# An mLSTM cell in front of a mixture layer: attention in halves of 64 tokens, in 64x64 quadrants of TensorE, with a state between the halves

## The chip, the cores and the metric

The kernel runs on one core of one Trainium2 chip. The metric is the device time in microseconds (us) of one execution; less is better. All times below come from one profiled execution of the kernel before, unless they are called a median.

## The reference

Two layers, one behind the other. The first is an mLSTM cell over 768 tokens, for 4 batches of 8 heads (32 pairs of batch and head) with head size 40:

```python
for t in range(S):
    m_new = np.maximum(f_gate[:, :, t] + m, i_gate[:, :, t])
    f_stab = np.exp(f_gate[:, :, t] + m - m_new)
    i_stab = np.exp(i_gate[:, :, t] - m_new)
    m = m_new
    C = f_stab[:, :, None, None] * C + i_stab[:, :, None, None] * np.einsum('bhd,bhe->bhde', vt, kt)
    n = f_stab[:, :, None] * n + i_stab[:, :, None] * kt
    h_tilde = np.einsum('bhde,bhe->bhd', C, qt)
    nq = np.einsum('bhd,bhd->bh', n, qt)[:, :, None]
    y[:, :, t] = o * h_tilde / np.maximum(np.abs(nq), 1.0)   # o = sigmoid(o_gate)
```

The second layer takes the 3072 tokens of 320 features (8 heads of 40):

```python
h = x @ w_in                                  # 320 -> 2048
out = (h * (1 / (1 + np.exp(-1.702 * h)))) @ w_out   # 2048 -> 320
```

The recurrence over tokens can be cut into windows. Within a window it is an attention with a causal mask and weights exp(...) from the gates; what came before the window enters through a state C (with n as a 41st column), which is brought forward once a window.

## The kernel before

**Windows.** There are 6 windows `w` of 128 tokens. A window has two stages. The *up* stage computes w_in times the tokens of all four batches (512 columns) for 16 blocks of 128 hidden features (`p_h`, L390 and L396) and applies the GELU on ScalarE (L401). The *down* stage multiplies by w_out: in window 0 straight, in 16 blocks (`p_out`, L417); from window 1 on as 14 products of a Strassen-like scheme (`down_fast`, L471), each 8 matmuls of 128x160, which needs sums of hidden blocks (`hidden_sums`, L452 to L456) and additions of the products into `o_sb` (L474, L476), all on VectorE.

**Attention.** The attention of window w+1 is spread over the down stage of window w, by `attention()`, one list of steps, and `stops`, the blocks behind which a step is issued. Each step serves one batch b (8 heads, as 4 pairs `p` of heads; head i of a pair lies in rows i*64 to i*64+39 of the transposed keys and queries):

- `columns`: the gate rows (`st`, from `gates`) are transposed by TensorE into columns `p_cols`, copied (L266) and put through exp (L267, L269); then the output gate's tanh (L271).
- `weights`: 8 exps on ScalarE (L305) over a tile `wt` into which `spread` has loaded the gate row from memory, one for each head; then the causal mask on POOL (L307, an affine select of 128x1024).
- `scores`: 8 matmuls K^T Q of 40 rows, two heads in the two row tiles of the array (`p_s`, L315), multiplied into `wt` by VectorE (L317).
- `values`: `p_o` = wt times V, 8 matmuls of 128x41 (L325), and `p_i` = Q times the state, 4 matmuls for pairs of heads (L330); VectorE scales and adds (L334, L335), divides and applies the gate (L338 to L344).
- `seam`: three transposes of the result (`p_x`, L353), copied by ScalarE into `xT` (L354), which the next up stage reads.

`carry` brings the state forward: POOL multiplies V by gate columns (`vw`, L360), TensorE multiplies by the keys (`p_c`, L364), POOL decays the old state (L371), VectorE adds (L375). It stands in the up stage of its own window, one batch behind each of the first four `j`. `transposes` of window w+1 stand behind the last four `j`: 8 TensorE transposes a batch (`p_t`, L279), keys copied by ScalarE and queries by VectorE (L281).

**Order.** Every engine runs its instructions in the order in which the program issues them (the schedule is written by hand), and waits in that order. So what stands behind a waiting instruction on an engine waits with it. All loads and stores go through SyncE's queue: `load` (L97), `load_gates` (L89), `fetch` (L137), `spread` (L287), stores (L422, L480). Products in float32 leave two records for each matmul in the profile, transposes one.

**Accumulators.** `ps_a` has four buffers of one bank, for all of attention; `ps_m` has four, for the mixture layer.

Of the kernel before, what the change touches and what calls it, by code (L numbers as in the profile page):

```python
# [17 lines left out]

L = 128
NEG = -1.0e30


# [7 lines left out]
def kernel(  # L34
# [24 lines left out]
    DH = DM // 2  # L59
    assert BH == 32 and D <= DP and DM == 320 and W == 512 and B == 4 and S % L == 0 and NF == 16  # L60
# [9 lines left out]
    ps_a = ctx.enter_context(tc.tile_pool(name="ps_a", bufs=4, space=PSUM))  # L70
# [7 lines left out]
    q_st = const.tile([L, BH, DP], FP, name="q_st")  # L78
    k_st = [const.tile([L, BH, DP], FP, name=f"k_st{i}") for i in range(2)]
# [6 lines left out]
    def load_gates(w):  # L86
        for dst, src in ((f_sb, f_gate), (i_sb, i_gate)):
            dst[w] = ld.tile([BH, L], FP, tag="fi", bufs=4, name="fi")
            nc.sync.dma_start(out=dst[w], in_=src[:, :, w * L:(w + 1) * L].rearrange("b h s -> (b h) s"))  # L89

    def load(w, what, bs=slice(0, B)):
        hs = slice(bs.start * H, bs.stop * H)
        for c in what:
            if c == "o" and w not in eo:
                eo[w] = ld.tile([L, BH, D], FP, tag="eo", bufs=1, name="eo")
            dst, src = {"k": (k_st[w % 2], k), "q": (q_st, q), "v": (v_st, v), "o": (eo.get(w), o_gate)}[c]
            nc.sync.dma_start(out=dst[:, hs, 0:D],  # L97
                              in_=src[bs, :, w * L:(w + 1) * L, :].rearrange("b h s d -> s (b h) d"))
# [39 lines left out]

    load_gates(0)
# [8 lines left out]

# [37 lines left out]
    for t in (k_st[0], q_st):  # L186
        G.memset(t[:, :, D:DP], 0.0)
# [3 lines left out]
    state = const.tile([128, BH // 2, 2, D1], FP, name="state")  # L191
# [5 lines left out]
    kT, qT, wt, ys, xT, gs, o_ps, sums = {}, {}, {}, {}, {}, {}, {}, {}  # L197
# [16 lines left out]
    def gates(w):  # L214
# [35 lines left out]
        V.tensor_scalar(out=st[BH:2 * BH, :], in0=m_run, scalar1=m, scalar2=None, op0=OP.subtract)  # L250
        V.tensor_scalar(out=st[2 * BH:3 * BH, :], in0=a, scalar1=end, scalar2=-1.0, op0=OP.subtract, op1=OP.mult)
        if 0 < w < NW - 1:
            dec[w] = gate.tile([BH, BH // 2], FP, name="dec")
            both = gate.tile([BH, 1], FP, name="both")
            V.tensor_tensor(out=both, in0=m, in1=end, op=OP.subtract)
            V.tensor_scalar(out=dec[w], in0=pair, scalar1=both, scalar2=None, op0=OP.mult)

    def columns(w):
        pt = ps_a.tile([L, 3 * BH + BH // 2], FP, tag="a", name="p_cols")
        T.transpose(pt[:, 0:3 * BH], stacked[w], ident[0:3 * BH, 0:3 * BH])  # L260
        n = 3 * BH
        if w in dec:
            n += BH // 2
            T.matmul(pt[:, 3 * BH:n], half.rearrange("p a b -> p (a b)"), dec[w], start=True, stop=True)
        c = cols[w] = gate.tile([L, 3 * BH + BH // 2], FP, name="cols")
# [8 lines left out]
    def transposes(w, b):  # L274
        for src, dst, name, copy in ((k_st[w % 2], kT, "kT", A.copy), (q_st, qT, "qT", V.tensor_copy if w else A.copy)):
            pt = ps_a.tile([128, NP, L], FP, tag="a", name="p_t")
            for p in range(NP):
                h = b * H + 2 * p
                T.transpose(pt[:, p, :], src[:, h:h + 2, :].rearrange("p a b -> p (a b)"), ident)  # L279
            dst[w, b] = work.tile([128, NP, L], FP, tag=name, bufs=4, name=name)  # L280
            copy(out=dst[w, b], in_=pt)  # L281

    def spread(w):

        for b in range(B):
            x = wt[w, b] = work.tile([L, NP, 2, L], FP, tag="wt", bufs=4, name="wt")
            nc.sync.dma_start(out=x.rearrange("s p i t -> s (p i) t"),  # L287
                              in_=m_row[w][b * H:(b + 1) * H, :].unsqueeze(0).to_broadcast([L, H, L]))

    def weights(w, b):  # L290
        if w == 0:
            x = wt[w, b] = work.tile([L, NP, 2, L], FP, tag="wt", bufs=4, name="wt")
            for i in range(2):
                pw = ps_a.tile([L, NP, L], FP, tag="a", name="p_w")
                T.matmul(pw, ident_b, neg_mask.unsqueeze(1).to_broadcast([L, NP, L]), start=True, stop=False)
                for p in range(NP):
                    h = b * H + 2 * p + i
                    one = pick[:, h:h + 1].to_broadcast([3 * BH, L])
                    T.matmul(pw[:, p, :], one, m3, start=False, stop=False)
                    T.matmul(pw[:, p, :], a3, one, start=False, stop=(p == NP - 1))  # L300
                A.activation(out=x[:, :, i, :], in_=pw, func=AF.Exp)
            return
        x = wt[w, b].rearrange("s p i t -> s (p i) t")
        for h in range(H):
            A.activation(out=x[:, h, :], in_=x[:, h, :], func=AF.Exp, scale=-1.0,  # L305
                         bias=cols[w][:, b * H + h:b * H + h + 1])
        G.affine_select(out=x, in_=x, compare_op=OP.is_ge, fill=0.0, base=0, pattern=[[0, H], [1, L]],  # L307
                        channel_multiplier=-1)

    def scores(w, b):  # L310
        pw = [ps_a.tile([L, NP, L], FP, tag="a", name="p_s") for _ in range(2)]
        for p in range(NP):
            for i in range(2):
                r = slice(i * 64, i * 64 + D)
                T.matmul(pw[i][:, p, :], kT[w, b][r, p, :], qT[w, b][r, p, :], start=True, stop=True)  # L315
        for i in range(2):
            V.tensor_tensor(out=wt[w, b][:, :, i, :], in0=pw[i], in1=wt[w, b][:, :, i, :], op=OP.mult)  # L317

    def values(w, b):
        hs = slice(b * H, (b + 1) * H)  # L320
        po = ps_a.tile([L, H, D1], FP, tag="a", name="p_o")
        for p in range(NP):
            for i in range(2):
                h = 2 * p + i
                T.matmul(po[:, h, :], wt[w, b][:, p, i, :], v_st[:, b * H + h, :], start=True, stop=True)  # L325
        u = po
        if w:
            pi = ps_a.tile([L, H, D1], FP, tag="a", name="p_i")
            for p in range(NP):
                T.matmul(pi[:, 2 * p:2 * p + 2, :].rearrange("p a b -> p (a b)"), qT[w, b][:, p, :],  # L330
                         state[:, b * NP + p].rearrange("p a b -> p (a b)"), start=True, stop=True)
            u = work.tile([L, H, D1], FP, tag="u", name="u")
            g = cols[w][:, BH + b * H:BH + (b + 1) * H].unsqueeze(2).to_broadcast([L, H, D1])
            V.tensor_tensor(out=u, in0=pi, in1=g, op=OP.mult)  # L334
            V.tensor_tensor(out=u, in0=po, in1=u, op=OP.add)  # L335

        den = work.tile([L, H, 1], FP, tag="den", name="den")
# [5 lines left out]
        y = ys[w, b] = work.tile([L, DM + 64], FP, tag="y", name="y")  # L343
        V.scalar_tensor_tensor(out=y[:, 0:DM].rearrange("p (h d) -> p h d", d=D), in0=z, scalar=0.5,  # L344
                               in1=den.to_broadcast([L, H, D]), op0=OP.mult, op1=OP.mult)
        G.tensor_copy(out=y[:, DM:DM + 64], in_=y[:, DM - 64:DM])

    def seam(w, b):
        if b == 0:
            xT[w] = work.tile([128, 3, B, L], FP, tag="xT", bufs=1, name="xT")  # L350
        px = ps_a.tile([128, 3, L], FP, tag="a", name="p_x")
        for c in range(3):
            T.transpose(px[:, c, :], ys[w, b][:, c * 128:(c + 1) * 128], ident)  # L353
        A.copy(out=xT[w][:, :, b, :], in_=px)  # L354

    def carry(w, b):
        hs = slice(b * H, (b + 1) * H)
        vw = work.tile([L, H, D1], FP, tag="vw", name="vw")
        e = cols[w][:, 2 * BH + b * H:2 * BH + (b + 1) * H].unsqueeze(2).to_broadcast([L, H, D1])
        G.tensor_tensor(out=vw, in0=v_st[:, hs, :], in1=e, op=OP.mult)  # L360
        pc = ps_a.tile([128, NP, 2, D1], FP, tag="a", name="p_c")
        for p in range(NP):
            h = b * H + 2 * p
            T.matmul(pc[0:64 + D, p].rearrange("p a b -> p (a b)"),  # L364
                     k_st[w % 2][:, h:h + 2, :].rearrange("p a b -> p (a b)")[:, 0:64 + D],
                     vw[:, 2 * p:2 * p + 2, :].rearrange("p a b -> p (a b)"), start=True, stop=True)
        ps = slice(b * NP, (b + 1) * NP)
        if w:
            d = cols[w][:, 3 * BH + b * NP:3 * BH + (b + 1) * NP].unsqueeze(2).to_broadcast([128, NP, 2 * D1])
            old = state[:, ps].rearrange("p j a b -> p j (a b)")  # L370
            G.tensor_tensor(out=old, in0=old, in1=d, op=OP.mult)  # L371
        for i in range(2):
            r = slice(i * 64, i * 64 + D)
            if w:
                V.tensor_tensor(out=state[r, ps, i, :], in0=pc[r, :, i, :], in1=state[r, ps, i, :], op=OP.add)  # L375
            else:
                V.tensor_copy(out=state[r, ps, i, :], in_=pc[r, :, i, :])
# [45 lines left out]

# [62 lines left out]


    def attention(w):
# [124 lines left out]
```

## Time and profile before

| | |
|---|---|
| median of 3 runs | 569.14 us (568.95 to 569.47) |
| span of the profiled execution | 567.2 us |
| median less that span | 2.0 us |
| TensorE busy | 557.2 us (98%) |
| VectorE, ScalarE, POOL busy | 254.8, 179.5, 64.4 us |
| up stage of window 1 (132.88 to 175.27) | 42.4 us |
| down stage of window 1 (175.27 to 223.9) | 48.6 us |

The span is the time from the first to the last instruction in the trace; 2.0 us of the measured time lie around it. The profile's parts that matter are the busy shares of the engines; the chain of work that ended last, which is followed back from the last instruction and is also given piece by piece in order of time; the timeline, which lists groups of instructions with their start, length and what ended the idle time before them; and the waits, which say in total which engine waited in front of which line, and for whom. PE is TensorE's matmul side, PEld its weight loads, DVE VectorE, ACT ScalarE, SP SyncE.

### The profile page before, as it was taken

The numbers are of one execution on the slowest core, as the hardware profiler recorded it, in microseconds if no ns is written. First come the engines' busy times: TensorE is split into PE (matmuls) and PEld (weight loads), VectorE is DVE, ScalarE is ACT, GpSimd is POOL, SyncE is SP. The second block draws the span as 40 slices with busy tenths as digits, with TensorE's granted clock in tenths as the row PEclk, the third lists the DMA queues.
The fourth block names the chain that finished last, engine by engine and source line by source line (L and its number), as shares of the span: only waits on it lengthen the run. The fifth ranks groups of instructions, "written<-read, shape, count | busy, mean of one in ns | idle before, by whom it ended". The sixth has DMA issues, their size and how long they took to land.

```text
span 567.2 us, 8277 instructions
## 1 busy us (share of the span) xinstructions
PE 557.2 (98%) x3282; PEld 401.7 (71%) x3282; DVE 254.8 (45%) x583; ACT 179.5 (32%) x387; POOL 64.4 (11%) x103
## 2 busy tenths in 40 slices
PE   8989999999999999999999999999999999999997
PEld 5844556885548998456999544899745699944697
DVE  6755869532645445016454314545302644400611
ACT  5544668102233420322610213441033262022200
POOL 5011001102400202100110210021210011000000
PEclk9979999999999999999999999999999999999999
DMA  9789699003654002581300392400342000000000
GB/s 167 148 263 206 167 304 110 1 23 72 150 92 50 24 1 51 73 189 22 39 13 1 72 219 23 49 24 2 71 94 102 0 13 13 12 14 0 0 24 24
DMA packets 111959, 41.45 MB, mean 73 GB/s; under 512 B 100624, under 2 KB 106800, under 8 KB 111920
## 3 DMA queue, kind: packets, MB, share of 16 engines
q1 hardware_dynamic: 111920, 40.92, 35.8%
q8 instruction: 26, 0.43, 0.3%
q14 instruction: 13, 0.11, 0.1%
HBM read 36.90 MB, written 4.01 MB: 72 GB/s over the span
## 4 chain that ended last, share of the span: by engine, by line
PE 88%; SPq 4%; DVE 3%; DMA 2%; ACT 1%; issue 1%; DVEq 0%; ACTq 0%
PE p_h L390 29%; PE p_out L471 28%; PE p_h L396 8%; PE p_o L325 6%; PE p_s L315 4%; PE p_out L417 4%; PE p_i L330 3%; PE p_t L279 3%; PE p_c L364 3%; SPq L137 2%; SPq L97 2%; PE p_x L353 1%; DMA bits<-in_moe_w_out_dram 1%; DVE w_out_sb L211 1%; DVE w_out_sb L209 1%
## 5 line engine op out<-in xcount | busy, mean ns | idle before, releaser
L390 PE MATMUL p_h<-xT,w_in_sb 128*128 128x512 f32 x384 | 178.2, 609 | 2.8 <-ACT xT L354 2.8
L390 PEld LDWEIGHTS p_h<-xT,w_in_sb 128*128 128x128 f32 x384 | 70.4, 192 | 94.5 <-issue 88.0
L401 ACT ACTIVATE g<-p_h 128x512 f32<-128x512 f32 x96 | 54.8, 596 | 147.7 <-PE p_h L396 86.3
L471 PE MATMUL p_out<-w_out_sb,g 128*128 128x160 f32 x480 | 70.5, 300 | 0.0
L471 PEld LDWEIGHTS p_out<-w_out_sb,g 128*128 128x128 f32 x480 | 66.7, 190 | 1.0 <-issue 0.5
L354 ACT COPY xT<-p_x 128x384 f32<-128x384 f32 x24 | 11.5, 478 | 148.8 <-PE p_x L353 148.8
L305 ACT ACTIVATE wt<-wt,cols 128x128 f32<-128x128 f32 x160 | 48.0, 392 | 0.0
L471 PE MATMUL p_out<-t,s 128*128 128x160 f32 x320 | 47.9, 303 | 0.0
L396 PE MATMUL p_h<-xT,w_in_x 64*128 64x512 f32 x192 | 47.7, 615 | 0.0
L325 PEld LDWEIGHTS p_o<-v_st,wt 128*128 128x128 f32 x384 | 45.0, 192 | 1.6 <-DVE wt L317 0.8
L325 PE MATMUL p_o<-v_st,wt 128*128 128x41 f32 x384 | 45.4, 278 | 0.6 <-DVE wt L317 0.6
L307 POOL TENSOR_SCALAR_AFFINE_SELECT wt<-wt 128x1024 f32<-128x1024 f32 x20 | 21.9, 1096 | 208.4 <-ACT wt L305 208.4
L476 DVE TENSOR_TENSOR o_sb<-o_sb,p_out 128x160 f32<-128x160 f32 x70 | 21.4, 317 | 53.8 <-PE p_out L471 53.6
L471 PEld LDWEIGHTS p_out<-t,s 128*128 128x128 f32 x320 | 44.2, 190 | 1.1
L281 DVE COPY qT<-p_t 128x512 f32<-128x512 f32 x20 | 13.7, 687 | 55.8 <-PE p_t L279 55.8
L375 DVE TENSOR_TENSOR state<-p_c,state 40x164 f32<-40x164 f32 x32 | 10.4, 326 | 60.2 <-PE p_c L364 59.5
L396 PEld LDWEIGHTS p_h<-xT,w_in_x 64*128 64x128 f32 x192 | 16.5, 186 | 29.5 <-issue 28.5
L317 DVE TENSOR_TENSOR wt<-p_s,wt 128x512 f32<-128x512 f32 x48 | 30.8, 682 | 12.9 <-POOL wt L307 9.6
L417 PE MATMUL p_out<-w_out_sb,g 128*128 128x320 f32 x128 | 36.3, 437 | 0.0
L334 DVE TENSOR_TENSOR u<-p_i,cols 128x328 f32<-128x328 f32 x20 | 10.0, 500 | 55.1 <-PE p_i L330 55.1
L417 PEld LDWEIGHTS p_out<-w_out_sb,g 128*128 128x128 f32 x128 | 23.7, 190 | 9.4
L315 PE MATMUL p_s<-qT,kT 40*128 40x128 f32 x384 | 27.9, 285 | 0.2 <-DVE wt L317 0.2
(118 smaller groups left out, 596.8 us busy)
## 6 DMA issues: line engine op xcount, KB each, us to landing
wt<-m_row SPq DMA_DIRECT2D x20, 512.0 KB, 6.6
bits<-in_moe_w_in_dram SPq DMA_DIRECT2D x8, 512.0 KB, 5.3
out_dram<-o_sb SPq DMA_DIRECT2D x24, 160.0 KB, 1.8
k_st<-in_k_dram SPq DMA_DIRECT2D x5, 640.0 KB, 9.2
q_st<-in_q_dram SPq DMA_DIRECT2D x5, 640.0 KB, 7.0
eo<-in_o_gate_dram SPq DMA_DIRECT2D x5, 640.0 KB, 5.4
v_st<-in_v_dram SPq DMA_DIRECT2D x5, 640.0 KB, 5.7
bits<-in_moe_w_out_dram SPq DMA_DIRECT2D x8, 320.0 KB, 5.3
```

Of the source, the lines that this page charges most:

```text
L279: T.transpose(pt[:, p, :], src[:, h:h + 2, :].rearrange("p a b -> p (a b)"), ident)
L305: A.activation(out=x[:, h, :], in_=x[:, h, :], func=AF.Exp, scale=-1.0, bias=cols[w][:, b * H + h:b * H + h + 1])
L307: G.affine_select(out=x, in_=x, compare_op=OP.is_ge, fill=0.0, base=0, pattern=[[0, H], [1, L]], channel_multiplier=-1)
L315: T.matmul(pw[i][:, p, :], kT[w, b][r, p, :], qT[w, b][r, p, :], start=True, stop=True)
L317: V.tensor_tensor(out=wt[w, b][:, :, i, :], in0=pw[i], in1=wt[w, b][:, :, i, :], op=OP.mult)
L325: T.matmul(po[:, h, :], wt[w, b][:, p, i, :], v_st[:, b * H + h, :], start=True, stop=True)
L390: T.matmul(ph[j][i], w_in_sb[:, c, f * 128:(f + 1) * 128], x[:, c, :], start=(first and c == 0), stop=(not first and c == 1))
L396: T.matmul(ph[j][i], w_in_x[r, j, :], x[r, 2, :], start=first, stop=not first)
L401: A.activation(out=g[:, i, :], in_=ph[j][i], func=AF.Gelu_apprx_sigmoid)
L417: T.matmul(po, gs[w, f // 2][:, f % 2, b * L:(b + 1) * L], w_out_sb[:, f, :], start=(f == 0), stop=(f == NF - 1))
L471: T.matmul(po, a(f), b[:, f, :], start=(f == 0), stop=(f == NH - 1))
L476: V.tensor_tensor(out=dst, in0=x, in1=po, op=OP.add)
```

## The change

Windows 1 to 5 are cut into halves `x` of 64 tokens. Within a half the attention is direct; the second half sees the first one through `state_mid`, a state between. All four products are now cut into 64x64: row tile by where the operands lie, column tile by the rows of the accumulator that are written. Steps serve `c`, two batches (16 heads, 8 pairs `j`), in place of one.

- **scores**: 64 matmuls a window, of 40 rows, 64 by 64 (64 keys, 64 queries of the same half). The tile `wt` has 64 columns a head in place of 128.
- **values**: `p_o` is 64 matmuls a window, each half by itself; `p_i` 64 matmuls, the first half against the old state, the second against `state_mid`.
- **carry**: 64 matmuls a window (32 in windows 0 and 5), which give both halves' contributions, `state_mid` first and then the next state. It is moved out of the up stage into the attention of its window, which is in the down stage of the window before, ahead of the second `weights`.
- **weights**: 32 exps a window of 128x64, 4 masks of 64x1024.
- **transposes** from window 2 on: keys and queries are loaded in another arrangement (`load_squares`, 8 transfers a window) so that VectorE's 32x32 transpose gives kT and qT directly, with 8 instructions of 128x512 a window. TensorE's transposes and both copies go. The keys are also loaded as before, for the carry.
- **buffers**: `ps_a` has two tiles of two banks in place of four of one; `state` has two copies. `spread` is four transfers to 64 partitions each, of half the bytes in all.
- **steps**: `at` says behind which block of the down stage each step is issued.

The core of the diff:

```diff
+    def load_squares(w):
+        for dst, src in ((k_sq, k), (q_sq, q)):
+            x = src[:, :, w * L:(w + 1) * L, :].rearrange("b (p two) (r c) d -> two r (b p) (c d)", two=2, c=4)
+            for i in range(2):
+                for n in range(2):
+                    r, at = slice(i * 64 + n * 32, i * 64 + n * 32 + 32), (1 - n) * 32
+                    nc.sync.dma_start(out=dst[r, at:at + BH // 2 * 4 * D].rearrange("r (j x) -> r j x", x=4 * D), in_=x[i])
...
     def transposes(w, b):
...
+        if w > 1:
+            at, n = 32 + b * NP * 4 * D, NP * 4 * D
+            for dst, src in ((kT, k_sq), (qT, q_sq)):
+                V.transpose(out=dst[w, b].rearrange("d j (r c) -> d j c r", c=4),
+                            in_=src[:, at:at + n].rearrange("r (j c d) -> r j c d", c=4, d=D)[:, :, :, 0:32])
+            return
...
-        x = wt[w, b].rearrange("s p i t -> s (p i) t")
-        for h in range(H):
+        x = wt[w, c].rearrange("s j i t -> s (j i) t")
+        for h in range(PH):
             A.activation(out=x[:, h, :], in_=x[:, h, :], func=AF.Exp, scale=-1.0,
-                         bias=cols[w][:, b * H + h:b * H + h + 1])
-        G.affine_select(out=x, in_=x, compare_op=OP.is_ge, fill=0.0, base=0, pattern=[[0, H], [1, L]],
-                        channel_multiplier=-1)
+                         bias=cols[w][:, c * PH + h:c * PH + h + 1])
+        for i in range(2):
+            r = x[i * HL:(i + 1) * HL]
+            G.affine_select(out=r, in_=r, compare_op=OP.is_ge, fill=0.0, base=0, pattern=[[0, PH], [1, HL]],
+                            channel_multiplier=-1)
...
+        for j in range(NJ):
+            b, p = 2 * c + j // NP, j % NP
             for i in range(2):
                 r = slice(i * 64, i * 64 + D)
-                T.matmul(pw[i][:, p, :], kT[w, b][r, p, :], qT[w, b][r, p, :], start=True, stop=True)
+                for x in range(2):
+                    t = slice(x * HL, x * HL + HL)
+                    T.matmul(pw[t, i, j * HL:(j + 1) * HL], kT[w, b][r, p, t], qT[w, b][r, p, t], start=True,
+                             stop=True)
...
+        def within(flip):
+            for j in range(NJ):
+                for x in range(2):
+                    t, i = slice(x * HL, x * HL + HL), x ^ flip
+                    T.matmul(po[t, i, j * D1:(j + 1) * D1], wt[w, c][t, j, i, :], v_st[t, c * PH + 2 * j + i, :],
+                             start=True, stop=True)
+
+        within(0)
+        for j in range(NJ):
+            b, p = 2 * c + j // NP, j % NP
+            for i in range(2):
+                r = slice(i * 64, i * 64 + D)
+                for x, s in enumerate((state[w % 2], state_mid)):
+                    t = slice(x * HL, x * HL + HL)
+                    T.matmul(pi[t, i, j * D1:(j + 1) * D1], qT[w, b][r, p, t], s[r, c * NJ + j, :], start=True,
+                             stop=True)
+        within(1)
...
+    def carry(w, c):
+        hs, js = slice(c * PH, (c + 1) * PH), slice(c * NJ, (c + 1) * NJ)
+        vw = work.tile([L, PH, D1], FP, tag="u", name="vw")
+        e = cols[w][:, 2 * BH + c * PH:2 * BH + (c + 1) * PH].unsqueeze(2).to_broadcast([L, PH, D1])
         G.tensor_tensor(out=vw, in0=v_st[:, hs, :], in1=e, op=OP.mult)
+        pc = banks("p_c")
+        halves = [slice(0, L)] if w == 0 else [slice(x * HL, x * HL + HL) for x in range(2 if w + 1 < NW else 1)]
+        for j in range(NJ):
+            for i in range(2):
+                for x, t in enumerate(halves):
+                    T.matmul(pc[i * 64:i * 64 + 64, x, j * D1:(j + 1) * D1], k_of(w)[t, c * PH + 2 * j + i, :],
+                             vw[t, 2 * j + i, :], start=True, stop=True)
...
+        old = state[w % 2]
+        for x, dst in enumerate((state_mid, state[1 - w % 2])[:len(halves)]):
+            d = cols[w][:, 3 * BH + x * BH // 2:3 * BH + (x + 1) * BH // 2][:, js]
+            G.tensor_tensor(out=dst[:, js], in0=old[:, js], in1=d.unsqueeze(2).to_broadcast([128, NJ, D1]), op=OP.mult)
+            V.tensor_tensor(out=dst[:, js], in0=new(x), in1=dst[:, js], op=OP.add)
+            old = dst
...
+    def attention(w):
+        at = (0, 1, 3, 6, 8, 10, 11, 13) if w == 1 else (0, 1, 2, 4, 6, 8, 9, 12)
+        calls = [[(columns, w)], [(weights, w, 0)], [(carry, w, 0), (carry, w, 1), (weights, w, 1)],
+                 [(scores, w, 0), (scores, w, 1)], [(values, w, 0)], [(values, w, 1)], [(seam, w, 0)], [(seam, w, 1)]]
+        return dict(zip(at, calls))
...
-                if j < B:
-                    carry(w, j)
-                else:
+                if j >= B:
                     transposes(w + 1, j - B)
```

## The prediction

> **What bounds the kernel now.** I read the page's busy shares, then the chain that ended last, then the chain in order of time, then the timeline of one start of a down stage, then the waits.
>
> ```profile
> PE 557.2 (98%) x3282; PEld 401.7 (71%) x3282; DVE 254.8 (45%) x583; ACT 179.5 (32%) x387; POOL 64.4 (11%) x103
> PE 88%; SPq 4%; DVE 3%; DMA 2%; ACT 1%; issue 1%; DVEq 0%; ACTq 0%
> 33.00:39.80 6.80, 6.23 (x10) 2.73 (x11) 4.39 (x8) 4.04 (x6) 1.61 (x3) 0.50 0.64 179
> ```
>
> TensorE is busy for 98% and is 88% of the chain, so a microsecond of TensorE work, or of TensorE waiting, is a microsecond of span. The third line (window, length, busy time and count of PE, PEld, DVE, ACT, POOL, granted clock) is the one disturbed stretch: at half clock.
>
> The chain in order of time gives the pieces that the change replaces:
>
> ```profile
> 34.44 6.34 PE p_h L390 x8
> 141.86 1.45 PE p_c L364 x16
> 173.53 1.75 PE p_t L279 x16
> 175.27 2.18 PE p_out L471 x16
> 177.85 6.72 PE p_out L471 x48
> 184.57 1.09 PE p_s L315 x16
> 185.66 4.54 PE p_out L471 x32
> 190.21 1.71 PE p_o L325 x16
> 191.92 0.93 PE p_i L330 x8
> 223.94 3.70 PE p_h L390 x8
> ```
>
> Columns: start, length, what, records; a matmul leaves two records, a transpose one. Nothing stands between the pieces; the one gap in a period is the 0.6 us before an up stage. Per record: p_o 107 ns, p_i 116, p_t 109, all with a stationary 128 wide; p_c 91, with 104 columns; the 41 columns that p_o streams don't show. So the stationary's width sets the pace of short matmuls. p_s, with two row tiles, has 68 ns; in its single records the matmuls start in pairs 6 ns apart, a pair every 105 ns or so: two row tiles overlap, but never more than one record of each.
>
> Now when the inputs of attention exist, from the timeline of a down stage's start:
>
> ```profile
> 180.94 0.18 DVE L266 COPY cols<-p_cols 128x32 f32<-128x32 f32 x1
> 181.19 1.28 ACT L267 ACT_TABLE_LOAD   x1 [5.68 <-DVE cols L266]
> 182.49 0.22 ACT L267 ACTIVATE cols<-p_cols 128x64 f32<-128x64 f32 x1
> 182.67 1.27 ACT L271 ACTIVATE eo<-eo 128x1280 f32<-128x1280 f32 x1
> 183.83 7.11 ACT L305 ACTIVATE wt<-wt,cols 128x128 f32<-128x128 f32 x24
> 186.34 1.09 POOL L307 TENSOR_SCALAR_AFFINE_SELECT wt<-wt 128x1024 f32<-128x1024 f32 x1 [37.00 <-ACT wt L305]
> 188.67 1.09 POOL L307 TENSOR_SCALAR_AFFINE_SELECT wt<-wt 128x1024 f32<-128x1024 f32 x1 [1.24 <-ACT wt L305]
> ```
>
> The stage begins at 175.27, the column copy ends 5.9 us later, the first mask only 12.2 us after the start. Before, the first TensorE reader of this is p_o at 190.21: the chain is hidden with little to spare. The waits say who sits idle:
>
> ```profile
> POOL wt L307 <- ACT wt L305: 208.4, 10, 40.8
> ACT L267 <- DVE cols L266: 22.7, 4, 5.7
> DVE wt L317 <- POOL wt L307: 9.6, 4, 2.7
> PE p_h L390 <- ACT xT L354: 2.8, 5, 0.6
> ```
>
> (total, times, longest). POOL waits for ScalarE before each first mask, harmless as long as no TensorE input stands behind that mask. The last row is the seam: TensorE waits 0.57 us for xT at each up stage.
>
> **What the Trainium skill says.** "TensorEngine Tiling (Array Packing)", Key Properties: tiles load weights and multiply independently, and a change of tiling mode drains the array. The trace agrees on both: paired starts in p_s, and p_s plus the two blocks after it are 5.63 us where 16 records at 56 ns and two blocks of 2.18 make 5.26, so the two mode changes cost some 0.4 us. "TensorE: Matmul & The Clock Gate", Part 3: matmuls start and end strictly in order, and a weight load overlaps running matmuls only in another row group. The pairs agree with the order: a record waits for the previous one of its own tile and holds up those behind it. Same page, Part 1: after an idle window of about 3.4 us the clock is halved. The trace's 0.50 from 33.0 to 39.8 follows idle spells of 0.83 and 0.57 us, so no run here shows a long one. "Vector Engine (DVE) Microarchitecture Reference", its 32x32 transpose mode: one element per cycle per lane; no row of before shows it.
>
> **The change, part by part (TensorE work).** Removed or rewritten for windows 1 to 5, in us: p_s 20 sections of 1.09 + 0.42 = 30.2; p_o and p_i 20 of 2.64 = 52.8; p_c (windows 0 to 4) 10 pieces of 1.45 = 14.5; p_t of windows 2 to 5, 8 pieces of 1.75 = 14.0. Sum 111.5.
>
> Added: 64x64 quadrants. p_s, p_o, p_i are 64 matmuls a window each, 5 x 384 = 1920 records; p_c is 64 matmuls for windows 1 to 4, 32 for windows 0 and 5: 640. In all 2560 records. A 64-wide record should take half of 107 = 54 ns on its tile, and two row tiles overlap: 27 ns a record, my choice. Bounds: 13 ns if all four quadrants overlap; 40 ns for p_s and p_i if two column tiles of one row group don't (of their eight records, in their written order, only two pairs then change row group: six slots of 54 ns for eight); 54 ns if nothing overlaps. At 27 ns: 69.1 us, and 0.42 for each of about 22 sections (5 scores, 10 values, 7 carries) 9.3: 78.4. **Net -33.1 us.**
>
> **The new wait.** The carry of window w moves from the up stage, where its inputs were ten microseconds old, to behind block 2 of the previous down stage. On POOL its first product (`vw`) stands behind the two masks of weights(0), these behind 16 exps, these behind cols. From D, the start of the down stage: the p_t pieces are gone, so the last GELU ends at D + 0.65; the last hidden sums on VectorE (2 x 0.66, then 4 x 0.60) end at 4.4, o_sb copy 0.32, cols copy 0.18: 4.85. Table load, exps of cols and dec, tanh: 2.9 from the copy's end to the first weight exp: 7.7. 16 exps of 128x64 at 0.24 (0.29 for 128 columns, less half a row): 11.5. Two masks of 1.09: 13.7. vw of 656 elements, twice the 0.73 of one of 328: **15.1**. TensorE has done p_cols and blocks 0 to 2 at D + 6.9: it waits 8.2 us. Behind it on TensorE stands everything: the second carry, eleven blocks, scores. The second carry waits again: vw(1) stands on POOL behind next(0), which needs VectorE's addition of mid(0): from the end of p_c(0) 0.5 + 0.75 + 1.45, with semaphores 3.1 us. Windows 2 to 4: 11.3 each, 34. Window 5, with one half only: 8.2 + 1.2. Window 1 (16 blocks in window 0's down stage, TensorE there at 88.9, vw at 93.3): 4.4 + 3.0, less 0.6 of an old wait. **Sum +50.1.** Bounds 42 to 58: with the exps at 0.20 to 0.29, and the masks at half price, since each covers 64 partitions.
>
> **Clock.** The half-clock stretch cost 6.34 - 3.70 = 2.6 us. An idle 8 us should bring one in each of five stages: **+13.2**; bounds 0 (clock kept) and 26 (both waits).
>
> **Seam.** seam 1 stands behind block 12, and block 13 (2.18) covers its copy: four waits of 0.57 go, **-2.3**. What is late next is nothing: hidden in block 13.
>
> **VectorE, POOL and queues.** VectorE loses four qT copies of 0.69 a window and gains eight transposes of 128x512, at 0.6 each (another 512-element row), bound above by 1.3 if their strided output halves the rate. They stand in the up stage, ahead of the hidden sums, with VectorE 45% busy: I take zero, and as the upper bound 3 us a window (12 in all) by which cols and so the first wait come later. ScalarE loses four kT copies and has as many exps of half the size (32 x 0.24 against 32 x 0.29). SP issues eight square loads a window instead of two, k twice, and spread in four transfers of half the bytes; they are due a whole stage ahead, in stretches whose DMA share is at most 0.6: zero, cover gone only if SP holds back stores, 1 to 2 us. Prologue: two more memsets, same products: zero, within 1 us.
>
> **Sum:** 567.2 - 33.1 + 50.1 + 13.2 - 2.3 = 595.1, and the median stands 2.0 above the profiled span: **597 us.**
>
> **Rivals.**
> 1. *Four quadrants at once (faster).* At 13 ns a record the products cost 33 + 9, 36 us less than above: 561 with the clock loss, 548 without. Place: every quadrant section. It decides below 16 ns (21 ns without a clock loss), where the saving pays for the waits. For it: the skill's independent tiles. Against: matmuls start in order, and the two records of a product sit next to each other on one tile, so only two tiles have work at once; p_s shows exactly two.
> 2. *Waits as worked out, clock kept.* 584. For it: seam waits of 0.57 leave 3.70 against 3.47, hardly a loss. Against: the stretch at 33 us.
> 3. *Supply of small products.* 40 ns for p_s and p_i adds 17: 614; all at 54 adds 69: 666. For it: nothing in the trace has column tiles. Against the latter: p_s's pairs.
> 4. *The change not doing what it says*, the carry covered as before: 567.2 - 33 - 2 + 2 = 534. It would need vw by D + 6.9, before the weight exps have begun. The POOL order forbids it.
>
> **Chances.** Forecast (clock lost, pace near 27) 0.48, rival 2 0.16, rival 3 0.13, rival 1 0.17, rival 4 0.06. A measurement of this kernel tells some 0.2% from no change. Rivals 1 and 4 give faster, less a sliver at the break-even: faster 0.22, same 0.02, slower 0.76. The range, 556 to 638, takes in rivals 1 with clock loss and 2, the 40 ns bound with late transposes; the forecast and rival 2 alone would be 580 to 615.
>
> **What would show it.** In the profile after: TensorE idle of 8 us behind block 2 of each down stage, released by POOL's vw, and 3 us before the second carry; TensorE's share down to about 90%; an up stage of 36 us without p_c and p_t; half clock behind each wait; the quadrant sections at 27 ns a record. It is wrong if TensorE runs through block 2 without idling, or if the quadrant rows show 15 ns or 50.

## The result, and the profile after

| | before | changed |
|---|---|---|
| median of the runs, us | 569.31 | 595.43 |
| ratio, with its 95% interval | | 1.0365 (1.0331 to 1.0399) |
| span of the profiled execution, us | 567.2 | 589.6 |

The change makes the kernel slower. Its four executions form two groups (589.5 and 591.3, 599.6 and 601.0); here, and in e3 and e7 below, the ratio leaves out the slower group, and the profile of the changed kernel belongs to the other.

Busy shares and the shares of the chain, from the page after:

```profile
PE 526.3 (89%) x4756; PEld 368.2 (62%) x4756; DVE 255.5 (43%) x511; ACT 160.9 (27%) x362; POOL 63.0 (11%) x88
PE 60%; issue 21%; DMA 7%; POOL 4%; ACT 4%; DVE 3%; SPq 0%; POOLq 0%; DVEq 0%
```

TensorE has 31 us less work in a span that is 22 us longer. It no longer carries the chain alone: parts of the chain now lie on POOL and ScalarE, and 21% of it is time ("issue") for which the profile shows no wait. The start of window 1's down stage (D = 190.1), from the timeline of the changed kernel, shows why:

```profile
194.86 0.18 DVE L286 COPY cols<-p_cols 128x32 f32<-128x32 f32 x1
195.12 1.28 ACT L287 ACT_TABLE_LOAD   x1 [4.27 <-DVE cols L286]
197.78 7.73 ACT L334 ACTIVATE wt<-wt,cols 128x64 f32<-128x64 f32 x32
201.76 2.35 POOL L338 TENSOR_SCALAR_AFFINE_SELECT wt<-wt 64x1024 f32<-64x1024 f32 x2 [56.14 <-ACT wt L334]
204.19 1.29 POOL L435 TENSOR_TENSOR vw<-v_st,cols 128x656 f32<-128x656 f32 x1
205.54 1.94 PE L441 MATMUL p_c<-vw,k_st 64*64 64x41 f32 x64 [8.18 <-POOL vw L435]
208.20 0.74 POOL L450 TENSOR_TENSOR state<-state_mid,cols 128x328 f32<-128x328 f32 x1 [2.02 <-DVE state_mid L451]
208.89 1.29 POOL L435 TENSOR_TENSOR vw<-v_st,cols 128x656 f32<-128x656 f32 x1
210.23 1.95 PE L441 MATMUL p_c<-vw,k_st 64*64 64x41 f32 x64 [2.75 <-POOL vw L435]
```

Read it as a staircase: copy, table load, 16 of the 32 exps, two masks, `vw`, and only then the first `p_c`, 8.18 us late; then VectorE's addition, the decay, the second `vw`, and the second `p_c`, 2.75 us late. The waits, in total:

```profile
PE p_c L441 <- POOL vw L435: 46.0, 9, 8.2
PEld p_t L307 <- ACT kT L308: 8.6, 7, 2.1
PE p_t L307 <- ACT kT L308: 7.5, 8, 1.8
```

The first row was forecast; the other two, which are the weight loads and the matmuls of the same transposes, were not. Of their 7.5 us, 4.7 lie in the start and 2.8 in window 0's up stage. Lengths of the stages, each from its first p_h or p_out to the next stage's, by the starts of single records (the last kernel is told below):

| us | before | changed | e8_busy_start |
|---|---|---|---|
| start, up to window 0's first p_h | 34.4 | 49.0 | 35.2 |
| up, window 0 | 45.1 | 45.7 | 45.1 |
| down, window 0 | 53.1 | 59.4 | 52.0 |
| up, windows 1 to 4, each | 42.4 to 42.5 | 35.9 | 35.9 |
| down, windows 1 to 4 | 48.8, 48.8, 48.8, 48.3 | 56.9, 55.9, 56.1, 53.1 | 43.4, 43.4, 43.5, 43.3 |

The up stages give 26 us, the down stages take 27 and window 0's 6, and the start takes 15.

### The profile page after: what moved, and what is told of

Its sections match the earlier page's. It is cut to its first block, busy times and chain, and to the rows that moved or that the text cites. A ratio compares the mean times of both kernels' runs of the same rounds, so it can differ in the third digit from the quotient of the medians.

```text
span 589.6 us, 11112 instructions
## 1 busy us (share of the span) xinstructions
PE 526.3 (89%) x4756; PEld 368.2 (62%) x4756; DVE 255.5 (43%) x511; ACT 160.9 (27%) x362; POOL 63.0 (11%) x88
## 4 chain that ended last, share of the span: by engine, by line
PE 60%; issue 21%; DMA 7%; POOL 4%; ACT 4%; DVE 3%; SPq 0%; POOLq 0%; DVEq 0%
PE p_out L540 23%; PE p_h L465 13%; DMA wt<-m_row 6%; PE p_out L492 5%; PE p_h L471 4%; PE p_c L441 3%; PE p_o L399 3%; POOL vw L435 2%; PE p_s L358 2%; PE p_i L409 2%; POOL wt L338 2%; PE p_s L347 1%; PE p_x L426 1%; PE p_t L307 1%; ACT wt L334 1%
## 5 line engine op out<-in xcount | busy, mean ns | idle before, releaser
L428 ACT COPY xT<-p_x 128x768 f32<-128x768 f32 (+1 forms) x14 | 9.9, 708 | 197.3 <-PE p_x L426 197.3
L524 DVE TENSOR_TENSOR s<-g 128x512 f32<-128x512 f32 x20 | 13.8, 689 | 99.9 <-ACT g L476 99.9
L338 POOL TENSOR_SCALAR_AFFINE_SELECT wt<-wt 64x1024 f32<-64x1024 f32 x20 | 23.0, 1150 | 275.4 <-ACT wt L334 274.7
L441 PE MATMUL p_c<-vw,k_st 64*64 64x41 f32 (+1 forms) x512 | 17.8, 297 | 37.0 <-POOL vw L435 37.0
L540 PEld LDWEIGHTS p_out<-t,s 128*128 128x128 f32 x320 | 49.5, 209 | 0.5
L471 PE MATMUL p_h<-xT,w_in_x 64*128 64x512 f32 x192 | 47.7, 615 | 0.0
L441 PEld LDWEIGHTS p_c<-vw,k_st 64*64 64x64 f32 (+1 forms) x512 | 16.4, 210 | 40.0 <-POOL vw L435 38.5
L334 ACT ACTIVATE wt<-wt,cols 128x64 f32<-128x64 f32 x160 | 38.8, 345 | 0.0
L471 PEld LDWEIGHTS p_h<-xT,w_in_x 64*128 64x128 f32 x192 | 16.5, 186 | 29.5 <-issue 28.7
L540 PE MATMUL p_out<-t,g 128*128 128x160 f32 x160 | 23.8, 302 | 0.0
L540 PE MATMUL p_out<-w_out_sb,s 128*128 128x160 f32 x160 | 23.4, 299 | 0.0
L399 PE MATMUL p_o<-v_st,wt 64*64 64x41 f32 x640 | 22.4, 228 | 0.0
```

What stands on the lines that cost most here:

```text
L338: G.affine_select(out=r, in_=r, compare_op=OP.is_ge, fill=0.0, base=0, pattern=[[0, PH], [1, HL]], channel_multiplier=-1)
L399: T.matmul(po[t, i, j * D1:(j + 1) * D1], wt[w, c][t, j, i, :], v_st[t, c * PH + 2 * j + i, :], start=True, stop=True)
L441: T.matmul(pc[i * 64:i * 64 + 64, x, j * D1:(j + 1) * D1], k_of(w)[t, c * PH + 2 * j + i, :], vw[t, 2 * j + i, :], start=True, stop=True)
L471: T.matmul(ph[j][i], w_in_x[r, j, :], x[r, 2, :], start=first, stop=not first)
L524: V.tensor_tensor(out=s1, in0=a10, in1=a11, op=OP.add)
L540: T.matmul(po, a(f), b[:, f, :], start=(f == 0), stop=(f == NH - 1))
```

## The experiments

### What holds up vw: e1_mask_behind

```diff
-        calls = [[(columns, w)], [(weights, w, 0)], [(carry, w, 0), (carry, w, 1), (weights, w, 1)],
+        calls = [[(columns, w)], [(weights, w, 0, "e")],
+                 [(carry, w, 0), (carry, w, 1), (weights, w, 0, "m"), (weights, w, 1)],
```

With "e" a step issues its exps alone, with "m" its masks alone.

> Only POOL's order changes: the two masks of weights(0) are issued behind the two carries instead of ahead of them. Theory (the masks, and through them the 16 exps, hold up vw): the first wait of TensorE for vw goes from 8.2 us to about 0.8 in the down stages of windows 1 to 4 and from 4.4 to about 0 in that of window 0; the second wait, behind VectorE's addition, stays at 2.7 to 4.6. Sum of waits 46 -> about 15 us, and with 5 to 13 us less lost at half clock the time falls from about 590 to 545-558. Rival (vw is late because the gate columns themselves are late: VectorE's sums and the table load): the first wait stays above 5 us and the time above 580.

Measured: 564.92 us, ratio to before 0.9913 (0.9885 to 0.9940). From the timeline of the same stage (here D = 196.3):

```profile
202.97 1.29 POOL L435 TENSOR_TENSOR vw<-v_st,cols 128x656 f32<-128x656 f32 x1 [51.10 <-ACT cols L289]
204.31 1.14 PE L441 MATMUL p_c<-vw,k_st 64*64 64x41 f32 x64 [0.71 <-POOL vw L435]
208.20 1.41 PE L441 MATMUL p_c<-vw,k_st 64*64 64x41 f32 x64 [2.75 <-POOL vw L435]
```

`vw` now starts on the gate columns, 6.7 us after D instead of 14.1, and the first wait is 0.7 us; in the stages of windows 0, 2, 3 and 4 it is gone. The second stays at 2.75 us in windows 1 to 3, as its own chain was not touched. In window 0's stage it grows from 4.6 to 7.3, because VectorE's addition to the state, on which it depends, waits its turn behind conversions of w_out (it starts at 117.90, 4.7 us after the first p_c has ended). The waits for vw fall from 46.0 to 16.5 us. The down stages of windows 1 to 4 lose 7 to 10 us each, 32 in all. The theory holds; late columns are not the cause. The time is above the forecast of 545 to 558 because the start took longer still in the profiled execution (first p_h at 55.3 us). This kernel is already 0.9% faster than before, by one change of order on POOL.

### What the long wait does to the clock: e4_keep_busy

```diff
+        if w > 1:
+            keep_busy(10 if c else 34)
         pc = banks("p_c")
```

> 34 and 10 idle bf16 matmuls of 512 columns (7.3 and 2.2 us) are put on TensorE ahead of the first and second p_c of windows 2 to 5, into the time in which it waits anyway. Theory (the long wait halves the clock): p_c takes 1.0 us per 64 matmuls' half instead of 1.95, the two products behind it 4.4 to 4.6 instead of 5.6 to 6.1; 2.5 to 3.5 us a window, the time falls by 10 to 14 us to 577-580. Rival (31 ns a record is p_c's own pace, by its order of tiles): p_c stays at 1.95 and the time within 4 us of 590.

Measured: 597.01 us (591.16 to 597.22). The median is above both bands, so the time by itself decides nothing. The stages do:

```profile
211.01 7.50 PE L165 MATMUL p_idle<-idle 128*128 128x512 bf16 x34
219.35 1.14 PE L442 MATMUL p_c<-vw,k_st 64*64 64x41 f32 x64 [0.83 <-POOL vw L434]
```

`p_c` takes 1.14 us in place of 1.94 with the same 64 records, so 31 ns was the half clock, not its pace. The down stages of windows 1 to 3 are 54.2, 53.3 and 53.3 us: 2.6 to 2.7 less each than in the changed kernel. In window 4's stage, where the changed kernel has no second wait, the idle matmuls cost nearly what is gained (52.7 against 53.1). The gain does not reach the total because of the start, which was 61.4 us in the profiled execution. Its code differs from the changed kernel's only in the accumulator tile of the idle matmuls, and p_o there takes 3.27 us for 16 records where the changed kernel's profile has 1.73 to 1.76: from 6.9 us on, that start ran at half pace. (The profile's clock row reads 1.00 in that stretch; the lengths of the records are the better witness.)

### Where the late start comes from: e2_prologue, e9_start_alone

Neither touches the attention from window 1 on. In e2, window 0's `p_w` are single banks:

```diff
-            pw = banks("p_w").rearrange("s i (p t) -> s i p t", t=L)
             for i in range(2):
+                pw = ps_m.tile([L, 1, NP, L], FP, tag="m", name="p_w")
```

> Only window 0's attention ahead of the first up stage changes: its p_w tiles come as single banks from ps_m, as p_idle does at each use, so that p_t and p_s have the two double tiles of ps_a for themselves. Theory (two double tiles make TensorE wait there for ScalarE's copies, the clock falls, and all behind is late): the first up stage starts at 35 to 38 us instead of 49, the time falls by 11 to 14 us to 577-580. Rival (the start is late because of the loads, their order on the queue, or POOL's additional memsets): the start stays at 47 to 49 us and the time at 590.

Measured: 588.38 us, ratio 1.0326 (1.0300 to 1.0352); first p_h at 42.9 us, 6.1 earlier, about half of what was expected, because one cause was left. The span is only 2.8 us shorter: window 0's up stage begins at half clock (40.9 to 47.7 us) and is 2.4 us longer. The same group of transposes in the start, before and in e2:

```profile
12.11 0.63 PE L279 MATMUL p_t<-ident,q_st 128*128 128x128 f32 x4
16.98 1.11 PE L306 MATMUL p_t<-ident,q_sq 128*128 128x128 f32 x4 [1.82 <-ACT kT L307]
```

The queries' transposes wait for ScalarE's copy of the keys. Keys and queries share one double tile, and the program keeps the order of dependencies for each tile, not each bank; e9 and e7, where the tiles are single, no longer have this wait in the start. The second row shows the next step as well: four transposes take 1.11 us in place of 0.63 once the clock has fallen. e9 gives `p_t` single banks too, and adds idle matmuls:

```diff
-        pt = banks("p_t")
...
+            pt = banks("p_t")[:, 0] if w else ps_m.tile([128, NP * L], FP, tag="m", name="p_t")
...
             weights(0, b)
+            keep_busy(2)
...
-    keep_busy(4)
+    keep_busy(7)
```

> The changed kernel with the start of e8 alone (single banks for p_w and p_t, idle matmuls); its attention from window 1 on is untouched. Theory (the start is a term of its own of some 15 us, as large as the missed part of the prediction): the first up stage at 33 to 35 us instead of 49, the time 573 to 577, still slower than before by the waits for vw. Rival (time gained at the start is given back, because window 1's loads and conversions then stand in the way): above 583.

Measured: 580.56 us, ratio 1.0183 (1.0152 to 1.0215); first p_h at 36.9 us. So the start is a term of its own: 12 us of it come back in the profile, 10 in the span. The first p_h is 2 us later than expected and the times lie 0.3 to 4.7 us above the band; the waits for vw are as they were (45.9 us).

### What VectorE's transposes are worth: e5_pe_transposes

```diff
-        if w > 1:
+        if False:                         # all windows by TensorE
...
-            if w + 2 < NW and i == (4 if w == 0 else 0):
-                load_squares(w + 2)
+            if w + 2 < NW and i == 4:
+                load(w + 2, "kq")
...
-                    load(w + 1, "v" if w == 0 else "vk")
+                    load(w + 1, "v")
```

> As the changed kernel, but keys and queries of windows 2 to 5 are loaded as before (behind block 4) and transposed by TensorE, copied by ScalarE and VectorE; no squares. Read by stage. Theory (transposes on TensorE cost their length, on VectorE nothing): the up stages of windows 1 to 4 grow from 35.9 to 39.4 us; the first wait for vw falls from 8.2 to 7.2, because the last GELU then ends 1.75 us earlier against the start of the down stage, less a query copy on VectorE: net +2.5 us a window, +10 in all. Rival (VectorE's transposes of 1.1 us delay the gate columns): the first wait falls by 3 us or more, and the sum of up and down stage stays within 0.5 us of the changed kernel's.

Measured: 627.90 us, ratio 1.1021 (1.0957 to 1.1085). Up stages of windows 1 to 4: 43.2 us, 7.3 more, not 3.5:

```profile
196.14 0.66 PE L307 MATMUL p_t<-ident,q_sq 128*128 128x128 f32 x4 [0.73 <-ACT kT L308]
```

The double tile costs here too: 0.7 us ahead of each of four groups, 2.9 us a stage; the transposes themselves take 4.4 in place of 3.5. The first wait for vw is 8.3 us against 8.2, so neither theory had that part: with or without its transposes, VectorE gives the columns no earlier relative to TensorE. In the changed kernel the transposes take this, from the groups of the page:

```profile
L300 DVE STREAM_TRANSPOSE kT<-k_sq 128x512 f32<-128x512 f32 x16 | 17.6, 1097 | 0.0
```

1.10 us each, between the bounds of 0.6 and 1.3, and hidden. This part of the change gains all that TensorE's transposes cost, 3.5 us a window in the kernel before.

### How quadrants overlap: e6_tile_runs

```diff
-        for j in range(NJ):
-            b, p = 2 * c + j // NP, j % NP
-            for i in range(2):
-                r = slice(i * 64, i * 64 + D)
-                for x in range(2):
-                    t = slice(x * HL, x * HL + HL)
+        for i in range(2):
+            r = slice(i * 64, i * 64 + D)
+            for x in range(2):
+                t = slice(x * HL, x * HL + HL)
+                for j in range(NJ):
+                    b, p = 2 * c + j // NP, j % NP
                     T.matmul(pw[t, i, j * HL:(j + 1) * HL], kT[w, b][r, p, t], qT[w, b][r, p, t], start=True,
                              stop=True)
```

> As the changed kernel, but the 32 matmuls of a scores step are ordered with the quadrant outermost: 8 matmuls (16 records) on one quadrant, then 8 on the next. The two records of a matmul are neighbours on one quadrant in both kernels. The prediction's premise (a record waits for the previous one of its tile and holds up those behind it): p_s goes from 2.0 us for 128 records to 6.9, 54 ns a record, +4.9 us a window. Rival (TensorE takes records of other tiles out of a queue behind a waiting one): 2.0 to 3.5 us, since runs of 16 records leave two to four quadrants within reach.

Measured: 634.76 us, ratio 1.1141 (1.1076 to 1.1207). The chain of this kernel, and its windows (columns as in the prediction) over the two blocks before p_s, p_s, and the two blocks after:

```profile
222.78 8.69 PE p_s L358 x128
```

```profile
217.30:222.70 5.40, 5.40 (x32) 5.23 (x32) 1.55 (x4) 0.00 (x0) 2.97 (x3) 0.82 0.00 0
222.80:231.40 8.60, 8.60 (x129) 8.48 (x129) 1.55 (x2) 0.00 (x0) 0.00 (x0) 0.69 0.01 2
231.50:238.40 6.90, 6.90 (x34) 6.73 (x36) 1.55 (x2) 0.00 (x0) 0.00 (x0) 0.65 0.06 24
```

In the changed kernel the same 128 records take 2.02 us: single records start in groups of four within 20 ns, a group every 58 ns, so all four quadrants work at once although the two records of one matmul are neighbours. In runs of 16 they start one every 58 ns, with a few overlapping pairs at each change of quadrant, and one every 107 ns from 3.4 us into the section on, where the clock falls though TensorE has not paused for 10 us; in the changed kernel, behind the same waits, it stays up there (58 ns a group to the end of the section, and 4.54 us for the two blocks behind). So the premise is half right: a quadrant takes one record every 58 ns, and a long run on it does hold up the others; but two records don't. The neighbours of a run reach past it by a few records. No run here takes weight loads and matmuls apart, so the mechanism stays open; the dependence on order does not.

### All causes taken away: e3_both, e7_single_p_t, e8_busy_start

In all three, `vw` and the first decay of both halves of the batches stand ahead of the masks on POOL, the second `p_c` has a block of its own, and the start has single banks for `p_w`:

```diff
-        at = (0, 1, 3, 6, 8, 10, 11, 13) if w == 1 else (0, 1, 2, 4, 6, 8, 9, 12)
-        calls = [[(columns, w)], [(weights, w, 0)], [(carry, w, 0), (carry, w, 1), (weights, w, 1)],
+        at = (0, 4, 5, 7, 9, 11, 12, 14) if w == 1 else (0, 3, 4, 6, 7, 9, 10, 12)
+        calls = [[(columns, w), (carry_v, w, 0), (carry_v, w, 1), (weights, w, 0, "e")],
+                 [(carry, w, 0), (weights, w, 0, "m")], [(carry, w, 1), (weights, w, 1)],
```

> The prologue's single banks as in e2, and in the attention both vw and the first decays ahead of all masks on POOL, the first p_c behind block 3, the second behind block 4, scores behind block 6, values behind 7 and 9, seams behind 10 and 12 (window 1: 4, 5, 7, 9, 11, 12, 14). Theory (waits for vw, the half clock behind them and the prologue are all that stands against the quadrants): waits for vw under 1 us in all, up stage at 35 to 38 us, p_c at 15 ns a record: 590 - 46 - 14 - 12 = 515 to 525. Rival (the quadrants need their inputs earlier than ScalarE and POOL can give them, so that the wait moves to scores or values): 540 or more, with TensorE idle ahead of p_s or p_o.

Measured: 543.39 us (535.18 to 545.07), ratio 0.9457 (0.9378 to 0.9537). The waits of TensorE for vw are gone from the list, p_c runs at full pace (but for one piece of 1.56 us), and the down stages of windows 1 to 4 are 43.3 to 43.9 us. But the time misses the band by 10 us and more, and the rival's sign, TensorE idle ahead of p_s, is there once: 4.3 us ahead of window 1's second p_s, behind VectorE's addition to the state. The rest is the start (43.0 us, p_t as in e2). Hence e7, with single tiles for `p_t` and, in window 1, at = (0, 4, 5, 8, 10, 12, 13, 14):

> As e3_both, but each p_t is a tile of its own (window 0: single banks of ps_m; window 1: one double tile each), and window 1's scores, values and first seam stand behind blocks 8, 10, 12 and 13 instead of 7, 9, 11 and 12. Theory (in a double tile the queries' transposes wait for the copy of the keys, since the two banks are one tile to the order of dependencies): the first up stage starts at 34 to 37 us instead of 43, and 4 us of waiting at window 1's second p_s go: 535-543 becomes 522-530. Rival (the start in e3_both is set by the loads or the conversion of w_in on VectorE, TensorE's waits there being slack): the start stays at 42 us or later and the time above 531.

Measured: 521.49 us (518.76 to 528.49), ratio 0.9147 (0.9116 to 0.9179). The median is half a microsecond below the band. The profiled execution, at 528.5 us, has its first p_h only at 39.9 us, with the clock at 0.50 from 25 to 40 us behind a wait of 0.57 us ahead of p_o. e8 puts idle matmuls there (the edit of e9):

> As e7_single_p_t, with two idle matmuls behind each weights step of window 0 and seven instead of four behind its columns. Theory (what spreads e7's times over 519 to 528 is the clock in the start: a wait of half a microsecond ahead of p_o can halve it for ten microseconds): the first up stage starts at 33 to 35 us at full clock in nearly all executions, times 517 to 521 with a spread under 3 us. Rival (the spread comes from the loads): the spread stays near 10 us, or the idle matmuls, 15 in all, delay the start by their 0.2 us each.

Measured: 521.63 us (519.76 to 524.03), ratio 0.9163 (0.9134 to 0.9192). First p_h at 35.2 us, clock 1.00 up to there; the spread is 4.3 us in place of 9.7, not under 3, and the median is e7's. The start accounts for 4.7 of the 7.4 us between the two profiled spans, and the stage behind it, which in e7 begins at half clock, for 1.1. So the clock explains most of that one execution; as one of six it says little of the spread, the rest of which stays open. This version and e7 are some 8% faster than before. In the chain of e8, the same place in the down stage of window 1 (D = 168.4):

```profile
170.98 6.72 PE p_out L553 x48
177.70 1.07 PE p_c L456 x64
178.77 2.37 PE p_out L553 x16
181.14 1.07 PE p_c L456 x64
182.22 4.54 PE p_out L553 x32
186.76 2.02 PE p_s L357 x128
```

Nothing stands between the pieces: TensorE alone carries this stretch again. One new wait is left elsewhere, in e7 and e8: 2.6 us in window 0's down stage, where p_c waits for the transfer of window 1's keys.

## Why the prediction was right, and where it was wrong

The mechanism that decided the sign was the right one. The forecast span of 595.1 us is 5.5 above the 589.6 of the profile. (That 597 lies within 2 us of the table's 595.43 says little, as that is the median of four times from 589.5 to 601.0.) Even the 5.5 are partly luck: two terms, the products and the start, were mis-sized by 17 and 14.5 us and cancelled. The quadrant sections of window 1's down stage, from the chain of the changed kernel:

```profile
217.76 2.02 PE p_s L358 x128
224.32 0.99 PE p_o L399 x29
225.38 0.93 PE p_i L409 x62
```

The terms of the prediction, one by one:

- **The new wait: right.** In window 1's down stage vw ends 15.4 us after D (15.1 in the working); the first wait is 8.2 us as forecast, the second 2.75 (3.1). In the stages of windows 2 to 4 the first wait is only 6.8: there ScalarE has done the table load, 1.28 us, before the columns come (at 283.68 in window 2's stage, where D = 282.9), so that it falls out of the staircase. Window 5 has no second wait, and window 0's stage has 4.4 and 4.6 (4.4 and 3.0). The sum is 46.0 (50.1 net, 50.7 before the old wait comes off). The lower bound "masks at half price" did not come: a mask of 64 partitions takes 1.15 us, one of 128 took 1.09. e1 shows that the masks and exps ahead of vw on POOL are the cause.
- **The clock: right in kind and roughly in size.** 13.2 us were put down. p_c at half pace costs 0.8 to 0.9 us in each of eight pieces and 1.7 in window 5's, and the blocks behind take 5.58, 5.92, 6.09 and 5.86 us where some 4.5 is full pace: some 14 us in all. e4, which takes it away directly, gives 2.6 to 2.7 us a stage in windows 1 to 3. One reading in the working is wrong: in the kernel before, the clock falls at 33.0 us, behind the wait of 0.83 us; the one of 0.57 comes after the fall.
- **The products: the step "two row tiles overlap: 27 ns a record, my choice" failed.** p_s has 15.8 ns a record, p_i 15, p_c 16.7 at full clock (1.07 us for 64). For p_o the step stands: its second piece has 32 records in 0.93 us, 29 ns, and its matmuls alternate between two quadrants only, those on the diagonal. The fault was to read "never more than one record of each" in p_s as a rule of order. That section has only two tiles, so it could not show what four do. Measured, the products take 10.1 us (p_s), 29 (p_o and p_i) and 22 (p_c, most of it at half clock), 61 in all; at full clock p_c would take 13, and all of them 52, where 2560 records at 27 ns were put at 69.1.
- **The start: the step "Prologue: two more memsets, same products: zero, within 1 us" failed.** It was +14.5 us. The change of `ps_a` to two double tiles was read for the down stages only. In window 0 it makes TensorE wait for ScalarE's copies and exps, 0.7 to 1.8 us at a time, 6.8 us more than before; behind these waits the clock reads 0.5 from 16.3 to 36.8 us, and the same work takes 7.8 us more. e2, e9 and e7 show it step by step; e9 adds idle matmuls, which keep the clock up.
- **The seam: right.** The wait for xT is 0.6 us in all, from 2.8.
- **VectorE's transposes: right.** 1.10 us each where 0.6 was taken, but nothing of it visible in the first wait.
- **The account.** By the starts of single records, with waits counted apart, the pieces that the change replaces fall from 104.8 to 60.8 us, by 44. The 111.5 us of the working is more by 8.4 us for changes of tiling mode at the 20 p_s; in the trace these stay in the blocks behind, before and after. With the waits for vw (46.0), the down stages' own blocks (7.9 longer, some 5 of it at half clock), the start (14.5), the rest of window 0's up stage (1.4: its transposes wait 2.8 us in the double tile, too, while 2.6 us of half clock that it had before are gone) and the seam (-2.3) this makes 23.5, against the 22.4 us between the spans. Changes of tiling mode are small: in e8, at full clock, the block behind a p_c takes 2.37 us where another takes 2.17, 0.2 us a section where 0.42 was put down.
- **The rivals.** Rival 1's price, four quadrants at once, came close (15 to 17 ns where 13 was put) for three of the four products. The sign held because p_o kept its 29 ns: the average is some 20 ns a record at full clock, above the 16 from which that rival decided. The start only added to it: e9, without it, is still 1.8% slower than before (1.0152 to 1.0215). Rival 3, that two column tiles of one row group don't overlap, falls with the 15.8 ns of p_s; window 5's p_c, which uses two such tiles alone, shows it directly: in e8 its 32 records start in pairs 7 ns apart, a pair every 58 ns, 1.06 us in all. Rival 2 (clock kept) falls with e4. Rival 4, vw by D + 6.9, is what e1 comes close to by moving the masks (vw ends at D + 8.0), and it then gives a kernel faster than before, though not its 534.

The Trainium skill's page "TensorE: Matmul & The Clock Gate", Part 3, lets weight loads overlap running matmuls only in another row group; the bound of 40 ns was built on it. The groups of four within 20 ns hold two quadrants of each row group, so that bound does not hold here; whether a load there overlaps a running matmul, no run here shows, as the ends of matmuls in the trace are modelled. "TensorEngine Tiling (Array Packing)", Key Properties (tiles work independently), fits, as long as the order alternates between tiles.

## What to carry to other kernels

When a step is moved ahead, follow its first input on every in-order queue down to what stands in front of it there: here a multiplication of 1.3 us stood behind 16 exps and two masks that it did not need, and moving those masks took away 30 us of waits. When buffers are merged, look at every stage that uses the pool, not only the one that was rewritten: two banks in one tile serialise a producer and a consumer that had a bank each. And read a pace from a section that has as many tiles as the one to be predicted, or carry both bounds into the forecast.

## What the runs showed of the hardware that was not expected

- Four 64x64 quadrants give 15 to 17 ns a record when consecutive matmuls alternate between them, two of them 29 to 33 (on the diagonal or in one row group), and runs of 16 records on one quadrant 58 at full clock.
- The clock can fall while TensorE is not idle: in e6's runs on one quadrant the mean clock was 0.69 in the section and 0.65 behind it, and the records went from 58 to 107 ns.
- A causal mask on POOL over 64 partitions took 1.15 us, over 128 partitions 1.09.
- Waits of 0.6 to 1.8 us in the start were followed by half clock for 10 us and more, and how long it lasted varied between the profiled executions: the first p_h came at 47, 49, 55 and 61 us in kernels that share that code (the last but for the tile of its idle matmuls). Why it varied stays open.
